# A dense product in Strassen form: units of 1024 tokens in place of 512, with half of each unit's squares kept and multiplied later

## The chip, the cores and the metric

The kernel runs on one core of one Trainium2 chip. The metric is the device time of one execution in microseconds (us); less is better. Four engines matter here: TensorE (PE, matmuls; its weight loads are shown apart as PEld), VectorE (DVE), ScalarE (ACT) and GpSimd (POOL). SyncE (SP) issues most transfers.

## The reference, cut to what matters

Three stages follow one another: a chunked attention, a mixture of experts that sends each token to one expert, and a dense feed-forward net over 3072 tokens. The change is in the third and in the few microseconds ahead of it.

```python
def _moe2_ref(x, w_in, w_out):        # x [3072, 512], w_in [512, 2048], w_out [2048, 512]
    h = x @ w_in
    r = np.maximum(h, 0.0)
    g = r * r
    return (g @ w_out).astype(np.float32)
```

## The kernel before, in words

Every large product is made in float32 precision from parts: an operand is split into a high part `hi` (a cast on ACT, L105) and a low part `lo` (a subtraction on DVE, L108), and a product is the three matmuls hi·hi, hi·lo and lo·hi (helper `split`).

**The experts.** A loop over slots `s` of 128 tokens (`for s in range(KE, NA)`, NA = 28) runs four groups of 12 matmuls a slot: `mm1(s+1, "a")`, `mm2(s, "a")`, `mm1(s+1, "b")`, `mm2(s, "b")`, with transposes (`htr`, `xtr`) between. Where a slot has another expert than the one before, the weights are split anew (`renew`). At the end of a slot `finish` scales the result (ACT, L1156) and GpSimd scatters its 128 rows to `y_d` in DRAM (L1157, indirect). Four times in a slot the loop calls `ffn_step`. In the last two slots (s = 26 and 27) each call takes one piece from the generator `ffn.run()`, so that the start of the third stage is woven into the experts. All queues run in the order in which the program issues; nothing is reordered later.

**The dense net.** The tokens, 24 tiles of 128 in expert order, are read back from `y_d` (`load_y`, L1257), transposed on PE (`ytr`, L1266), and multiplied by `w_in` in one level of Strassen's scheme: both operands are cut in quarters, seven products of sums of quarters replace eight. The tokens' seven sums (`sums`, L1279) are split into `yc1` to `yc7` (`ycw`). The weights' seven sums have been made and split earlier and lie in DRAM (`wi_d`); they are read back for each use (L1322).

Before, a unit `u` has 512 tokens (`NU` = 6), and a step (u, d), d from 0 to 3, makes 512 columns of the hidden layer. One of its seven products is 12 matmuls with 256 columns in the moving operand (L1313): two halves `jj` by two `kt` by three parts. The results lie in four PSUM banks X, Y, Z and W. ACT and DVE add them up (L1373 to L1401: `c1`, `u2`, `v`, `c2`), take `max(h,0)*h` (L1398, L1403) and split the square into `g` (`split_g`). `second(u, d, half)` then multiplies `g` by `w_out` (`mm2`, L1338 to L1340: 24 matmuls of 512 columns), one step behind the products, into four PSUM banks `acc`, one for each 128 tokens. After the last step of a unit `evict` copies them out, and GpSimd scatters the rows to `out` (L1360).

**Weights of the second product.** `w_out` comes as float64 and is converted in 32 pieces by `Convert`; each piece takes four DVE instructions (L190 to L199) and a split. Half of them are made in the experts' stage, and 16 are made after it, one at every second piece of the generator (`conv.step()`), so in the first four steps.

**The seam.** Between the experts and the dense net stands a branch, `tc.If(cnt > NA)` (L1603), for extra slots that these inputs do not need.

Of the kernel before, what the change touches and what calls it, by code (L numbers as in the profile page):

```python
# [21 lines left out]
def kernel(  # L22
# [33 lines left out]
    NU = NT // 4  # L56
# [1106 lines left out]
    class Ffn:  # L1163
# [3 lines left out]
        def __init__(self, wout, conv):  # L1167
            self.wout, self.conv = wout, conv
            self.w, self.yc, self.ys, self.yb, self.src, self.g, self.z = {}, {}, {}, {}, {}, {}, {}
            self.acc = None  # L1170
            self.out = []
# [26 lines left out]
        def combine(self, d, blocks):  # L1198
# [10 lines left out]
            def make(i):  # L1209
                t = self.w[i] = self.big.tile([P, 2, 2, 256], F32R, name="ww", tag=f"w{i}")  # L1210
                hi, lo = (t[:, x].rearrange("p k f -> p (k f)") for x in range(2))
                split(hi, lo, src[i])
                return t

            def store(i):
                r0 = (7 * d + i - 1) * P
                nc.sync.dma_start(out=wi_d[r0:r0 + P, :], in_=self.w[i].bitcast(F32).rearrange("p a k f -> p (a k f)"))
                return None
# [31 lines left out]
        def bank(self, b):  # L1250
            t = self.z[b] = self.ps.tile([P, 2, 256], F32, name="z" + b, tag="z" + b)
            return t

        def load_y(self, u, j):
            pool, tag = (moe.xp, "mx") if u == 0 or j < 2 else (moe.yp, "ysb")
            t = pool.tile([P, DM], F32R, name="ys", tag=tag)
            nc.sync.dma_start(out=t.bitcast(F32), in_=y_d[(4 * u + j) * P:(4 * u + j + 1) * P, :])  # L1257
            self.ys[u, j] = t

        def ytr(self, u, t):  # L1260
            for h in range(2):
                z = self.bank(("XY", "ZW")[h][t])
                for i in range(2):
                    for kt in range(2):
                        kk = 2 * h + kt
                        nc.tensor.transpose(  # L1266
                            z[:, kt, i * P:(i + 1) * P].bitcast(F32R),
                            self.ys[u, 2 * t + i][:, kk * P:(kk + 1) * P], identr,
                        )
                if (u, h) not in self.yb:  # L1270
                    pool, tag = (wres["1a"], ("wh1a1", "wl1a1")[h]) if u == 0 else (holds["2b"], f"r2b{h}")
                    self.yb[u, h] = pool.tile([P, 2, 512], F32, name="yb", tag=tag)
                nc.scalar.copy(out=self.yb[u, h][:, t], in_=z.rearrange("p a b -> p (a b)"))

        def sums(self, u):
            (b11, b12), (b21, b22) = ((self.yb[u, h][:, 0], self.yb[u, h][:, 1]) for h in range(2))
            t1, t2, t3, t4 = (self.big.tile([P, 512], F32, name=f"t{j}", tag=f"t{j}") for j in range(1, 5))
            for o, a, b in ((t1, b12, b11), (t2, b22, t1), (t3, b22, b12), (t4, b21, t2)):
                nc.vector.tensor_tensor(out=o, in0=a, in1=b, op=ALU.subtract)  # L1279
            self.src = {1: b11, 2: b21, 3: b22, 4: t4, 5: t1, 6: t2, 7: t3}  # L1280

        def ycw(self, *which):
            for i in which:
                t = self.yc[i] = self.big.tile([P, 2, 2, 256], F32R, name="yc", tag=f"yc{i}")
                hi, lo = (t[:, x].rearrange("p k f -> p (k f)") for x in range(2))
                split(hi, lo, self.src[i])

        def prep(self):
            self.load_y(0, 0)
            self.load_y(0, 1)  # L1290
            yield "load"
            self.ytr(0, 0)
            self.load_y(0, 2)
            self.load_y(0, 3)
            yield "x"
            self.ytr(0, 1)
            yield "x"
            self.sums(0)
            self.ycw(1, 6)
            yield "x"  # L1300
            self.ycw(5, 7)
            yield "x"
            self.ycw(2, 3, 4)
            yield "x"

        def product(self, u, d, i, b, start):
            z = self.bank(b) if start else self.z[b]
            w, y = self.w[i], self.yc[i]
            for jj in range(2):
                c = slice(jj * P, (jj + 1) * P)  # L1310
                for kt in range(2):
                    for x, (wx, yx) in enumerate(((0, 0), (0, 1), (1, 0))):
                        nc.tensor.matmul(  # L1313
                            out=z[:, jj, :], lhsT=w[:, wx, kt, c], rhs=y[:, yx, kt, :],
                            start=start and (jj, kt, x) == (0, 0, 0), stop=(jj, kt, x) == (1, 1, 2),
                            skip_group_check=True,
                        )
            if (u, d) != (NU - 1, ND - 1):
                d1 = (d + 1) % ND
                t = self.w[i] = self.big.tile([P, 2, 2, 256], F32R, name="ww", tag=f"w{i}")  # L1320
                r0 = (7 * d1 + i - 1) * P
                nc.sync.dma_start(out=t.bitcast(F32).rearrange("p a k f -> p (a k f)"), in_=wi_d[r0:r0 + P, :])  # L1322
            return z.rearrange("p a b -> p (a b)")

        def split_g(self, half, src):
            g = [wres["1a"].tile([P, 2, 2, 256], F32R, name="g", tag=f"w{x}1a{half}") for x in "hl"]
            split(*(z.rearrange("p t j c -> p (t j c)") for z in g), src.rearrange("p t c -> p (t c)"))
            self.g[half] = g

        def mm2(self, d, half, j):  # L1330
            gh, gl = self.g[half]
            t, c = j // 2, slice(j % 2 * P, (j % 2 + 1) * P)
            for jj in range(2):
                wt = self.wout[4 * d + 2 * half + jj]
                wh, wl = wt[:, 0], wt[:, 1]
                a, b_ = gh[:, t, jj, c], gl[:, t, jj, c]
                s0, s1 = (d, half, jj) == (0, 0, 0), (d, half, jj) == (ND - 1, 1, 1)
                nc.tensor.matmul(out=self.acc[j], lhsT=a, rhs=wh, start=s0, stop=False)  # L1338
                nc.tensor.matmul(out=self.acc[j], lhsT=a, rhs=wl, start=False, stop=False)  # L1339
                nc.tensor.matmul(out=self.acc[j], lhsT=b_, rhs=wh, start=False, stop=s1)  # L1340

        def second(self, u, d, half):
            if (d, half) == (0, 0):
                self.acc = [
                    pool.tile([P, DM], F32, name=f"acc{j}", tag=tag)
                    for j, (pool, tag) in enumerate(((moe.ps_h, "h"), (moe.ps_y, "y"), (moe.ps_t, "tr"), (moe.ps_t, "tr")))
                ]
            if u == 0:
                self.conv.until(8 * ND + 2 * (4 * d + 2 * half + 2))
            for j in range(4):  # L1350
                self.mm2(d, half, j)

        def evict(self, u, j):
# [5 lines left out]
            jj = 4 * u + j  # L1359
# [6 lines left out]

        def step(self, u, d):
# [293 lines left out]
```

## Time and profile before

| | |
|---|---|
| Three runs | 996.0, 999.01 and 999.05 us; median 999.01 us |
| The profiled execution | 998.1 us, of which the profile's span is 996.4 us |
| PE busy over the span | 957.3 us (96%) |
| DVE, ACT, POOL busy | 608.1, 396.6, 164.7 us |
| First matmul of a Strassen product | 475.7 us after the start of the span |
| Granted TensorE clock | 1.00 nearly throughout (2.4 GHz); 0.50 is 1.2 GHz |

Matmuls are pipelined: the time that one takes is longer than the distance to the next. What a stream of them costs is read from start to start in the timeline.

### The profile page before, as it was taken

Reading aid. Unit: us, or ns where it says so; the run is one execution under the profiler, and the core shown is the slowest. Engines: PE = TensorE matmul, PEld = TensorE weight load, DVE = VectorE, ACT = ScalarE, POOL = GpSimd, SP = SyncE. Lnnn points to the kernel's source line nnn. Section 1 sums busy time; section 2 is a strip of 40 time slices with the busy share of each in tenths; the row PEclk is TensorE's granted clock in tenths of the full one; section 3 lists DMA queues with packets and bytes.
Section 4 is the critical chain, followed back from the end, with each engine's and each line's share of the span. In section 5 each row is a group of like instructions: output and inputs, shape, how many; then the busy total and the mean of one; then the engine's idle time right before and its main releaser. Section 6 shows DMA issues by size and latency. Waiting matters only on the chain.

```text
span 996.4 us, 19267 instructions
## 1 busy us (share of the span) xinstructions
PE 957.3 (96%) x6990; PEld 827.1 (83%) x6990; DVE 608.1 (61%) x1163; ACT 396.6 (40%) x701; POOL 164.7 (17%) x197
## 2 busy tenths in 40 slices
PE   6889799999999999999999999999999999999997
PEld 5667577888887887877889999989989989899996
DVE  7777795647757677885797543633654454455333
ACT  8656533635546465675434212211321211132111
POOL 8765212121211111210000010010000001001001
PEclk9999799999999999999999999999999999999999
DMA  8993716554857677895895574575556557545621
GB/s 328 349 407 138 253 37 229 191 169 128 308 188 279 210 267 250 311 336 206 313 345 173 190 252 155 190 267 165 174 195 228 180 180 244 195 153 189 219 79 43
DMA packets 74600, 217.11 MB, mean 218 GB/s; under 512 B 8436, under 2 KB 8564, under 8 KB 74496
## 3 DMA queue, kind: packets, MB, share of 16 engines
q1 hardware_dynamic: 55488, 166.50, 47.8%
q0 software_dynamic: 8640, 28.32, 8.0%
q10 hardware_dynamic: 10368, 20.98, 6.3%
q8 instruction: 57, 0.93, 0.4%
q14 instruction: 47, 0.39, 0.1%
HBM read 257.70 MB, written 38.80 MB: 298 GB/s over the span
## 4 chain that ended last, share of the span: by engine, by line
issue 66%; DMA 15%; POOL 2%; POOLq 0%
DMA y_d<-ysb,sidx 15%; POOL out_dram L1360 2%; POOLq L1657 0%; POOLq L1031 0%; POOLq L1360 0%; POOLq L1157 0%; POOLq L1603 0%
## 5 line engine op out<-in xcount | busy, mean ns | idle before, releaser
L1340 PE MATMUL acc<-wo,g 128*128 128x512 f32 x384 | 149.9, 390 | 0.0
L1339 PE MATMUL acc<-wo,g 128*128 128x512 f32 x384 | 149.7, 390 | 0.0
L1338 PE MATMUL acc<-wo,g 128*128 128x512 f32 x384 | 149.5, 389 | 0.0
L1360 POOL DMA_INDIRECT out_dram<-osb,oid x24 | 25.5, 1062 | 485.1 <-ACT osb L1356 475.3
L1397 DVE TENSOR_TENSOR cf<-zY,v 128x512 f32<-128x512 f32 x24 | 16.6, 690 | 137.6 <-PE zY L1313 137.6
L105 ACT CAST g<-cf 128x1024 fp32r<-128x1024 f32 x48 | 50.6, 1054 | 118.2 <-DVE cf L1398 68.5
L108 DVE TENSOR_TENSOR g<-cf,g 128x1024 fp32r<-128x1024 f32 x48 | 58.8, 1225 | 60.6 <-ACT g L105 60.6
L1394 ACT COPY cf<-zX 128x512 f32<-128x512 f32 x24 | 14.1, 587 | 200.6 <-PE zX L1313 200.6
L1340 PEld LDWEIGHTS acc<-wo,g 128*128 128x128 f32 x384 | 72.1, 188 | 15.2
L1338 PEld LDWEIGHTS acc<-wo,g 128*128 128x128 f32 x384 | 72.3, 188 | 13.4
L1339 PEld LDWEIGHTS acc<-wo,g 128*128 128x128 f32 x384 | 72.1, 188 | 13.4
L1157 POOL DMA_INDIRECT y_d<-ysb,sidx x28 | 33.5, 1195 | 273.3 <-ACT ysb L1156 208.7
L1313 PEld LDWEIGHTS zX<-yc,ww 128*128 128x128 f32 x576 | 74.6, 189 | 3.5
L1313 PE MATMUL zY<-yc,ww 128*128 128x256 f32 x576 | 76.9, 283 | 0.0
L1313 PE MATMUL zW<-yc,ww 128*128 128x256 f32 x576 | 76.9, 283 | 0.0
L1313 PE MATMUL zX<-yc,ww 128*128 128x256 f32 x576 | 76.6, 282 | 0.0
L1313 PEld LDWEIGHTS zY<-yc,ww 128*128 128x128 f32 x576 | 72.6, 192 | 0.1
L1313 PEld LDWEIGHTS zW<-yc,ww 128*128 128x128 f32 x576 | 72.6, 192 | 0.0
L135 POOL COPY kw<-kt 64x672 f32<-64x672 f32 x62 | 51.5, 831 | 10.5 <-PE sp L277 8.2
L1108 PE MATMUL yps<-wh2a,hTha 128*128 128x512 f32 x112 | 46.2, 412 | 0.3 <-ACT ysb L1156 0.3
L108 DVE TENSOR_TENSOR hTlb<-tr,hThb 128x512 fp32r<-128x512 f32 x28 | 19.3, 689 | 43.1 <-ACT hThb L105 42.6
L1108 PE MATMUL hps<-wh1b,xT 128*128 128x512 f32 x104 | 42.9, 413 | 1.8 <-ACT ha L1125 1.8
(313 smaller groups left out, 2058.3 us busy)
## 6 DMA issues: line engine op xcount, KB each, us to landing
ww<-wi_d SPq DMA_DIRECT2D x161, 512.0 KB
r1a<-in_moe_w_dram SPq DMA_DIRECT2D x54, 512.0 KB
r1b<-in_moe_w_dram SPq DMA_DIRECT2D x54, 512.0 KB
r2a<-in_moe_w_dram SPq DMA_DIRECT2D x52, 512.0 KB
r2b<-in_moe_w_dram SPq DMA_DIRECT2D x52, 512.0 KB
wi_d<-ww SPq DMA_DIRECT2D x28, 512.0 KB
vb<-in_v_dram SPq DMA_DIRECT2D x32, 390.0 KB
rw<-in_moe_w_in_dram ACTq DMA_DIRECT2D x32, 256.0 KB
```

Of the source, the lines that this page charges most:

```text
L105: nc.scalar.copy(out=hi, in_=src)
L108: eng.tensor_tensor(out=lo, in0=src, in1=hi.bitcast(F32), op=ALU.subtract)
L135: (nc.vector if eng == "v" else nc.gpsimd).tensor_copy(out=out, in_=in_)
L1108: nc.tensor.matmul(out=out_ps, lhsT=ah, rhs=wh, start=first, stop=False)
L1157: nc.gpsimd.indirect_dma_start(out=y_d[:, :], out_offset=bass.IndirectOffsetOnAxis(ap=sidx[:, s:s + 1], axis=0), in_=y, in_offset=None, bo ...
L1313: nc.tensor.matmul(out=z[:, jj, :], lhsT=w[:, wx, kt, c], rhs=y[:, yx, kt, :], start=start and (jj, kt, x) == (0, 0, 0), stop=(jj, kt, x) ...
L1338: nc.tensor.matmul(out=self.acc[j], lhsT=a, rhs=wh, start=s0, stop=False)
L1339: nc.tensor.matmul(out=self.acc[j], lhsT=a, rhs=wl, start=False, stop=False)
L1340: nc.tensor.matmul(out=self.acc[j], lhsT=b_, rhs=wh, start=False, stop=s1)
L1360: ins = nc.gpsimd.indirect_dma_start(out=out[:, :], out_offset=bass.IndirectOffsetOnAxis(ap=oid[:, jj:jj + 1], axis=0), in_=o, in_offset=N ...
L1394: nc.scalar.copy(out=c1[:, 0], in_=z)
L1397: nc.vector.tensor_tensor(out=c1[:, 1], in0=z, in1=v, op=add)
```

## The change

1. A unit has 1024 tokens (`NU` = 3), and a step makes 256 columns of the hidden layer (128 of each half), so there are eight steps a unit and 24 in all, as before. A product is 6 matmuls with 512 moving columns (no `jj` loop), 168 products in all, as before.
2. A step's square has two token halves. The first is multiplied by `w_out` a step later, as before (`second`, 12 matmuls each). The second is kept in SBUF as float32 (`keep`, `kept`). After the eight steps `rest` splits the kept pieces one by one into two buffers and multiplies them: 16 pieces of 12 matmuls, in the same four PSUM banks.
3. The weights of two steps lie in one tile, so `wi_d` is read at every second step.
4. Transposes and sums of the next unit are made in `rest`, in two halves `r` (`ytr(u+1, r)`, `ycw(r)`), straight from PSUM; for the first unit they are made in the last two slots of the experts.
5. For that, the loop over slots takes the generator's first piece (the eight loads of `y_d`, issued on SP) at the end of slot 25, ahead of what slot 26 issues there, and then one piece a call: the transposes of r = 0 at the first call in slot 26, eleven sums and splits over the other three, the transposes of r = 1 at the first call in slot 27, and so on. No product is left in the experts' loop (before, two were).
6. The tiles for `w_out` get other places in SBUF; five in place of six are loaded at the first of the two places in slot 27.

```diff
-    NU = NT // 4
+    NU = NT // 8
...
+        def ycw(self, r):
+            b11, b12, b21, b22 = (self.b[h, t] for h in range(2) for t in range(2))
...
+            return [
+                lambda: nc.scalar.copy(out=tmp_tile("t1", "u2"), in_=b12),
+                lambda: sub(tmp_tile("t3", "v"), b22, tmp["t1"]),
+                lambda: sub(tmp["t1"], tmp["t1"], b11),
+                put(1, b11), put(7, "t3"), put(5, "t1"),
+                lambda: sub(tmp_tile("t2", "v"), b22, tmp["t1"]),
+                put(2, b21), put(6, "t2"),
+                lambda: sub(tmp_tile("t4", "u2"), b21, tmp["t2"]),
+                put(3, b22), put(4, "t4"),
+            ]
 
         def prep(self):
...
             self.load_y(0, 0)
             self.load_y(0, 1)
             yield "load"
...
+            for r in range(2):
+                self.ytr(0, r)
+                ops = self.ycw(r)
+                yield "x"
+                for n in (4, 4, 4):
+                    for _ in range(n):
+                        ops.pop(0)()
+                    yield "x"
 
         def product(self, u, d, i, b, start):
             z = self.bank(b) if start else self.z[b]
             w, y = self.w[i], self.yc[i]
-            for jj in range(2):
-                c = slice(jj * P, (jj + 1) * P)
-                for kt in range(2):
-                    for x, (wx, yx) in enumerate(((0, 0), (0, 1), (1, 0))):
-                        nc.tensor.matmul(
-                            out=z[:, jj, :], lhsT=w[:, wx, kt, c], rhs=y[:, yx, kt, :],
...
-            if (u, d) != (NU - 1, ND - 1):
...
+            for kt in range(2):
+                for x, (wx, yx) in enumerate(((0, 0), (0, 1), (1, 0))):
+                    nc.tensor.matmul(
+                        out=z, lhsT=w[:, d % 2, wx, kt], rhs=y[yx][:, kt, :],
...
+            if d % 2 and (u, d) != (NU - 1, 2 * ND - 1):
...
+            kept = (c1[:, 1], c2[:, 1]) if last else self.keep(d)
+            relu2(kept[0], c1[:, 1])
+            self.split_g(1, c2[:, 0])
+            relu2(kept[1], c2[:, 1])
...
+        def rest(self, u):
+            D, nxt = 2 * ND, u + 1 < NU
+            order = [(D - 1, 0), (D - 1, 1)] + [(d, half) for d in range(D - 1) for half in range(2)]
+            n = len(order)
+            self.second(u, D - 1, 0)
+            self.split_g(0, self.kept[order[0]])
+            for j in range(4):
+                self.mm2(1, D - 1, 1, j, False, True)
+                self.evict(u, 0, j)
+            self.split_g(1, self.kept[order[1]])
+            yield "x"
+            self.open_acc()
+            ops = []
+            for k in range(0, n - 2):
+                for j in range(4):
+                    self.mm2(k % 2, *order[k], j, k == 0, False)
+                self.split_g(k % 2, self.kept[order[k + 2]])
+                if nxt and k in (0, 7):
+                    r = int(k > 0)
...
+                    self.ytr(u + 1, r)
+                    ops = self.ycw(r)
...
+                else:
+                    for _ in range(2):
+                        if ops:
+                            ops.pop(0)()
+                yield "x"
+            for j in range(4):
+                for k in (n - 2, n - 1):
+                    self.mm2(k % 2, *order[k], j, False, k == n - 1)
+                self.evict(u, 1, j)
...
-            if s < NA - 2:
+            if s < NA - 3 or (s == NA - 3 and n < 2):
                 return
+            n = 1
...
             moe.mm2(s, "b")
-            ffn_step(1)
+            ffn_step(2)
```

## Rows read from the trace of the kernel before

**Rows 1.** The page: busy time of the engines, share, instructions.

```profile
PE 957.3 (96%) x6990; PEld 827.1 (83%) x6990; DVE 608.1 (61%) x1163; ACT 396.6 (40%) x701; POOL 164.7 (17%) x197
```

**Rows 2.** Busy time by stretch: length, then PE, PEld, DVE, ACT, POOL, clock, DMA.

```profile
457.30:483.50 26.20, 23.46 (x125) 18.98 (x123) 15.66 (x21) 15.63 (x27) 3.48 (x3) 1.00 0.70 241
483.50:508.00 24.50, 24.46 (x176) 23.25 (x177) 19.25 (x42) 7.47 (x15) 0.00 (x0) 1.00 0.91 348
568.00:650.00 82.00, 82.00 (x525) 74.61 (x524) 40.54 (x49) 19.71 (x29) 4.32 (x4) 1.00 0.61 204
896.00:990.00 94.00, 94.00 (x574) 84.59 (x573) 37.64 (x43) 17.40 (x24) 5.82 (x6) 1.00 0.38 131
```

**Rows 3.** Groups of instructions by shape, whole span (busy us, mean ns, idle before).

```profile
L1340 PE MATMUL acc<-wo,g 128*128 128x512 f32 x384 | 149.9, 390 | 0.0
L1313 PE MATMUL zY<-yc,ww 128*128 128x256 f32 x576 | 76.9, 283 | 0.0
L1313 PE MATMUL zZ<-yc,ww 128*128 128x256 f32 x288 | 38.5, 283 | 1.5 <-PEq L1603 1.5
L105 ACT CAST yc<-t 128x512 fp32r<-128x512 f32 x24 | 14.2, 620 | 6.8 <-DVE t L1279 6.7
L108 DVE TENSOR_TENSOR wl2a<-r2a,wh2a 128x1024 fp32r<-128x1024 f32 x16 | 18.8, 1217 | 2.4 <-ACT wh2a L105 2.4
```

**Rows 4.** Timeline of PE, two products and the matmuls behind them (start, us).

```profile
599.94 1.60 PE L1313 MATMUL zZ<-yc,ww 128*128 128x256 f32 x12
601.38 1.60 PE L1313 MATMUL zW<-yc,ww 128*128 128x256 f32 x12
603.51 0.39 PE L1338 MATMUL acc<-wo,g 128*128 128x512 f32 x1
...
605.55 0.39 PE L1338 MATMUL acc<-wo,g 128*128 128x512 f32 x1
```

**Rows 5.** Timeline and waits of SP's queue ahead of the loads of `y_d`.

```profile
458.96 0.55 SPq L1015 DMA_DIRECT2D r2b<-in_moe_w_dram  x2
461.52 0.35 SPq L1257 DMA_DIRECT2D ys<-y_d  x1
...
SPq L1257 <- DMA y_d<-ysb,sidx: 1.8, 1, 1.8
```

**Rows 6.** Timeline of PE in slots 26 and 27.

```profile
460.38 0.48 PE L1108 MATMUL yps<-wh2a,hTha 128*128 128x512 f32 x1
464.21 0.36 PE L1266 MATMUL zX<-identr,ys 128*128 128x128 f32 x2 [0.37 <-DMA ys<-y_d]
464.91 0.37 PE L1266 MATMUL zX<-identr,ys 128*128 128x128 f32 x2 [0.33 <-DMA ys<-y_d]
465.12 0.51 PE L1266 MATMUL zZ<-identr,ys 128*128 128x128 f32 x4
465.46 0.46 PE L1108 MATMUL hps<-wh1b,xT 128*128 128x512 f32 x1
483.54 1.66 PE L1313 MATMUL zZ<-yc,ww 128*128 128x256 f32 x12 [1.46 <-PEq L1603]
```

**Rows 7.** Timeline of DVE: two splits, one after the other; one converted piece.

```profile
479.46 0.69 DVE L108 TENSOR_TENSOR yc<-yb,yc 128x512 fp32r<-128x512 f32 x1
480.06 0.68 DVE L108 TENSOR_TENSOR yc<-t,yc 128x512 fp32r<-128x512 f32 x1
498.37 0.42 DVE L108 TENSOR_TENSOR wo<-wf,wo 128x256 fp32r<-128x256 f32 x1
500.03 0.69 DVE L1377 TENSOR_TENSOR u<-zY,cf 128x512 f32<-128x512 f32 x1
```

**Rows 8.** Timeline of PE behind an idle stretch, and a stretch's clock there.

```profile
152.73 0.50 PE L1108 MATMUL hps<-wh1b,xT 128*128 128x512 f32 x1 [1.81 <-ACT ha L1125]
154.50:155.00 0.50, 0.50 (x2) 0.39 (x2) 0.50 (x2) 0.00 (x0) 0.00 (x0) 0.50 1.07 418
157.50:158.00 0.50, 0.50 (x13) 0.50 (x12) 0.00 (x0) 0.18 (x1) 0.00 (x0) 0.84 1.05 389
```

More of the change, by code (lines that the diff above doesn't have):

```diff
@@ L1260, in ytr, with tiles, load_y @@
-        def ytr(self, u, t):
+        def tiles(self, r):
+            return [4 * t + 2 * r + i for t in range(2) for i in range(2)]
+        def load_y(self, u, r):
+            for n, j in enumerate(self.tiles(r)):
+                if u:
+                    t = (moe.xp if n < 2 else moe.yp).tile([P, DM], F32R, name="ys", tag="mx" if n < 2 else "ysb")
+                elif n % 2 == 0:
+                    kind = ("1a", "1b")[r]
+                    pair = holds[kind].tile([P, 2, DM], F32R, name="ys", tag=f"r{kind}{n // 2}")
+                    t = pair[:, 0]
+                else:
+                    t = pair[:, 1]
+                nc.sync.dma_start(out=t.bitcast(F32), in_=y_d[(8 * u + j) * P:(8 * u + j + 1) * P, :])
+                self.ys[u, j] = t
@@ L1270, in ytr @@
[L1270 to L1286, printed above, removed]
+                        for i in range(2):
+                            kk = 2 * h + kt
+                            nc.tensor.transpose(
+                                z[:, kt * 256 + i * P:kt * 256 + (i + 1) * P].bitcast(F32R),
+                                self.ys[u, 4 * t + 2 * r + i][:, kk * P:(kk + 1) * P], identr,
+                            )
@@ L1330, in mm2 @@
[L1330 to L1340, printed above, removed]
+            for kt in range(2):
+                for x, (wx, yx) in enumerate(((0, 0), (0, 1), (1, 0))):
+                    nc.tensor.matmul(
+                        out=z, lhsT=w[:, d % 2, wx, kt], rhs=y[yx][:, kt, :],
+                        start=start and (kt, x) == (0, 0), stop=(kt, x) == (1, 2),
+                        skip_group_check=True,
+                    )
@@ new lines, in windex, with mm2 @@
+        def windex(self, d, half):
+            return 4 * (d // 2) + 2 * half + d % 2
+        def mm2(self, n, d, half, j, first, last):
+            g, wt, c = self.g[n], self.wout[self.windex(d, half)], slice(j * P, (j + 1) * P)
+            nc.tensor.matmul(out=self.acc[j], lhsT=g[:, 0, c], rhs=wt[:, 0], start=first, stop=False)
+            nc.tensor.matmul(out=self.acc[j], lhsT=g[:, 0, c], rhs=wt[:, 1], start=False, stop=False)
+            nc.tensor.matmul(out=self.acc[j], lhsT=g[:, 1, c], rhs=wt[:, 0], start=False, stop=last)
@@ L1423, in run @@
         def run(self):
+            self.kept = {}
             yield from self.prep()
             for u in range(NU):
-                for d in range(ND):
+                for d in range(2 * ND):
                     yield from self.step(u, d)
-            self.second(NU - 1, ND - 1, 0)
-            for j in range(4):
-                self.mm2(ND - 1, 1, j)
-                self.evict(NU - 1, j)
-            yield "x"
+                yield from self.rest(u)
     with tc.manual_schedule():
```

162 lines of the change are left out of this document (80 added, 82 removed).

## The prediction

> **What bounds the kernel now.** Read the page's first part first: PE is busy for 96% of the span, DVE for 61%, ACT for 40% [rows 1]. Then look where that share is full. By stretch, PE is busy in every microsecond of the dense net, from the first product behind the branch to the last matmul, and the clock is at its upper level; DVE is half idle there, except in the first 25 us, where it is busy for 19.25 of 24.5 us [rows 2]. So in the dense net only what PE issues counts, as long as no other engine comes late. The stretch ahead of it, the last two slots of the experts, is the one with holes: 23.46 of 26.2 us [rows 2], with waits for loads of `y_d` and for the branch [rows 6]. The change touches both: it shortens the issue in the full stretch and reorders the one with holes.
>
> What a product costs is read from start to start in the timeline, not from the mean durations, which overlap [rows 3]. Twelve 256-column matmuls take 601.38 - 599.94 = 1.44 us, 120 ns each; nine of 512 columns take 605.55 - 603.51 = 2.04 us, 227 ns each [rows 4]. Two small ones cost 240 ns, one large one 227 ns.
>
> **The products.** 2016 matmuls of 256 columns (three groups of 576 and one of 288, [rows 3]) become 1008 of 512. A product goes from 1.44 us to 6 x 0.2267 = 1.36 us; 168 products save 168 x 0.08 = 13.4 us. No row has a 512-column matmul with `yc` and `ww`, but those with `g` and `wo` have the same type, shape and a weight load each, so I take their distance. The bounds are no gain (0, if weight loads still set the pace) and 13.4 us. `second` and `rest` together keep the 1152 matmuls of before (3 x 384), and the 96 transposes stay 96.
>
> Here a rule of the Trainium skill speaks against the gain: "TensorE: Matmul & The Clock Gate", section "Back-to-back issue gap", gives an isolated matmul N / 2.4 ns and a fixed part of about 2.5 ns. By that rule 1008 fewer matmuls would save an estimated 1008 x 2.5 ns = 2.5 us. The rows give a fixed part of 2 x 120 - 227 = 13 ns, so the trace does not agree, and the sum goes by the rows.
>
> **The loads of `y_d` move ahead.** They wait for the scatter of slot 25: SP's loads begin at 461.52, after a wait on that scatter [rows 5]. That is no earlier in the new order, since the scatter is not. But PE reaches the transposes earlier: in the new order they stand where `mm2(26, "a")` stands now, at 460.38, and the first tile was there at 464.21, the second at 464.91 [rows 6]. The half r = 0 needs four tiles; at 0.7 us each the fourth comes at 464.2 + 3 x 0.7 = 466.3. Eleven transposes follow it, at 0.34 / 4 us each (465.12 to 465.46, [rows 6]), so PE goes on at 467.3. That is 6.9 us for 1.36 us of work: a stall of 5.5 us. Moving the eight loads also delays what SP issues next, the reload of `r2b` (458.96 now, [rows 5]), to about 465; it is split only in slot 27, 15 us later, so it costs nothing unless it needs over 10 us to land.
>
> **The sums of both halves fall into the experts' loop.** Before, these slots hold 11 DVE instructions for the first unit (four sums, seven splits); now they hold two lots of 11, with one copy and seven casts each on ACT. DVE needs 0.60 us from one to the next (480.06 - 479.46, [rows 7]). PE's order from 467.3: three groups of 12 matmuls at 12 x 0.2267, some 2.8 us with their starts, and two lots of transposes at 0.35 us; it reaches the transposes of r = 1 at 476.5. These write the banks that the sums of r = 0 still read. DVE's order: the split for `htr(27, "a")` at 471.3, three instructions and a put (0.6 x 4 = 2.4), the weights `wl2a` (two at 1.2, [rows 3]), then seven more up to the last reader of bank W (4.2): 480.2. So PE waits about 2.7 us in the midst of these transposes and goes on at 480.5. Two groups of the experts follow (5.5 us, to 486.0), then the branch, where PE sat 1.46 us [rows 6]: the first product starts at 487.5. By then DVE has done the first split of r = 1 (about 485.8) and reaches that for the second product at 488.8, just in time.
>
> Now compare equal work. At 483.54 the kernel before had two products behind it (2.9 us) and 16 transposes fewer (1.34 us). The seam thus costs 487.5 - 483.54 + 2.9 - 1.34 = 5.5 us. The bounds are 2.8 us, if DVE is not late at the second transposes, and about 8 us, if the second loads or the reload are late too.
>
> **The clock.** PE idles 3.8 us before the first tile, and again 2.7 us. Behind an idle 1.81 us at 152.73 the granted clock stood at 0.50 from about 154.2 until about 157.7 [rows 8]: 3.5 us at the lower level, a loss of 1.75 us of full-rate work. Behind the 1.46 us at the branch it stayed at 1.00 [rows 2]. I take 1.3 us for the first gap, because a part of the slow time falls on waiting anyway, and 1.0 for the second (little over an even chance of 1.75): 2.3 us, between 0 and 5.
>
> **Conversions and squares in the first unit.** A step has now 11 DVE instructions of 512 elements, 6.6 us, and five conversions a step, each 500.03 - 498.37 = 1.66 us [rows 7]: 14.9 us, against 7 x 1.36 + 24 x 0.2267 = 15.0 us of PE. Before it was 20.5 us of PE for a little more work. The first step has no `second`: 9.5 us of PE against 6.6 + 3 x 1.66 = 11.6 us of DVE. DVE falls some 2 us behind and does not catch up before the conversions end in the fourth step. PE needs DVE's sums of the products 6 and 7 only behind `second`, some 4 to 5 us later, so most of the lag is covered. I take 1.0 us, between 0 and 6 (all that DVE can lose to casts queued on ACT behind a wait).
>
> **`rest`.** While PE does 12 matmuls (2.72 us), DVE has one split and up to two sums or splits (1.8 us); ACT up to three casts of 0.62 us [rows 3], under 1.9 us. The split of piece k+2 starts when piece k is multiplied, and has the 2.72 us of piece k+1 to get ready; it takes about 1.4 us. Hidden, cover 1.3 us a piece. The transposes for the next unit wait for loads issued some 50 us (r = 0) or seven pieces (r = 1) earlier: nothing. The reads of `wi_d` halve, and each has a whole step to land: nothing. Evictions and the tail behind the last matmul have the same form: nothing.
>
> **Sum.** -13.4 + 5.5 + 2.3 + 1.0 = -4.6 us. From the profiled execution's 998.1 us that is 993.5 us (span about 992); the median of the runs shown stands 0.9 us above that execution, so 994.4 us.
>
> **The rivals.**
> 1. *The seam is cheap.* DVE is not late at the second transposes and the clock holds: 2.8 us in place of 5.5 and 2.3, nothing in the first unit. -13.4 + 2.8 gives 988.4 us. For it: the clock has held through 1.46 us idle. Against it: 3.8 us idle is more than twice the stretch behind which it fell. Chance 0.19.
> 2. *DVE bounds the first unit.* The 14.9 against 15.0 us leave no room for bubbles, and ACT's casts stand behind copies that wait for PE. With 1.2 us lost in each of the four steps beyond the forecast's 1.0, the time is 999.2 us, no change. Against it: DVE may lag 4 to 5 us first. Chance 0.14.
> 3. *`rest` is not covered (slower).* If the split and the two sums of a piece run as a chain, cast (0.62), then subtraction (0.69), three times, a piece takes 3.9 in place of 2.72 us. It decides from 0.32 us for each of the 24 pieces in the two units that prepare another (7.6 us undo the gain and the 0.3%); at the full 1.2 us the time is 1023 us, at a third of it 1004. Against it: ACT can cast ahead while DVE subtracts, as the two successive splits 0.60 us apart show [rows 7]. Chance 0.08.
> 4. *The wide product is no faster.* If the columns alone set the pace, a 512-column matmul costs as much as two narrow ones and the 8.8 us of the seam, the clock and the first unit remain: 1007.8 us. By the fixed part that the section of the Trainium skill's page "TensorE: Matmul & The Clock Gate" cited above gives, the time would be an estimated 1005.3 us. Against it: 227 ns stands for all 1152 matmuls of `second` in this trace, 13 ns under two narrow ones. Chance 0.03.
>
> **How the numbers follow.** The forecast has 0.56, with its own range 991 to 997.5. About 0.3% (3 us) is what a measurement of this kernel can tell from no change. Faster by more (under 996): most of the forecast (0.47) and rival 1, 0.66. Within: the rest of the forecast and rival 2, 0.23. Slower: rivals 3 and 4, 0.11. A range of 989 to 999.5 us leaves out half of rival 1 and rivals 3 and 4, about 0.2.
>
> **What would show it.** Right: products at 1.36 us from start to start; a PE wait for `ys` of 3 to 6 us near 460 and one for DVE near 478; a clock under 1.00 behind the first; the first product at 487 to 491; no PE wait in `rest`; a last matmul near 986. Wrong: products at 1.44 us (rival 4), PE waits for `g` on DVE or ACT beyond 600 us (rival 3), PE waits for `u2`, `cf` or `g` over 5 us in all in the first four steps (rival 2), or a clock of 1.00 all through the seam (rival 1).

## The result and the profile after

The changed kernel takes 1008.31 us (median of seven runs, 1005.85 to 1010.84), the one before 999.05 us (seven runs, 996.0 to 1003.65): a ratio of 1.0089, 95% interval 1.0063 to 1.0115. It is 0.9% slower. The forecast was 994.4 us with a range up to 999.5; the time lies outside.

The profiled execution has a span of 1006.6 us against 996.4 before. First the page's busy times of the changed kernel, the answer to [rows 1]:

```profile
PE 956.9 (95%) x5982; PEld 778.7 (77%) x5982; DVE 622.1 (62%) x1259; ACT 397.3 (39%) x731; POOL 162.6 (16%) x197
```

The 1008 matmuls that were to go have gone, yet PE is busy as long as before: what was saved in number was lost again in slower matmuls. The span grew by waits. The waits of PE from slot 26 to the fourth step (line, releaser, us in total, times, longest):

```profile
PE zX L1277 <- DMA ys<-y_d: 3.9, 2, 3.6
PE zZ L1277 <- DVE tu L1291: 3.5, 1, 3.5
PE zX L1336 <- PEq L1662: 2.5, 1, 2.5
PE zY L1277 <- DMA ys<-y_d: 2.4, 2, 2.1
PE zW L1336 <- DVE cf L1418: 0.9, 2, 0.5
PE tr L1132 <- ACT hb L1125: 0.3, 1, 0.3
```

The kernel before waited 0.9 us there for `y_d` and 1.46 us at the branch. The timeline of PE there (start, us, idle before), the answer to [rows 6]:

```profile
455.45 0.39 PE L1108 MATMUL hps<-wh1a,xT 128*128 128x512 f32 x1
...
462.34 0.37 PE L1277 MATMUL zX<-identr,ys 128*128 128x128 f32 x1 [3.56 <-DMA ys<-y_d]
463.02 0.62 PE L1277 MATMUL zX<-identr,ys 128*128 128x128 f32 x3 [0.31 <-DMA ys<-y_d]
465.75 0.37 PE L1277 MATMUL zY<-identr,ys 128*128 128x128 f32 x1 [2.10 <-DMA ys<-y_d]
...
467.85 0.76 PE L1108 MATMUL yps<-wh2a,hTha 128*128 128x512 f32 x1
...
483.56 0.72 PE L1277 MATMUL zZ<-identr,ys 128*128 128x128 f32 x4 [3.55 <-DVE tu L1291]
...
494.73 0.47 PE L1336 MATMUL zX<-yc,ww 128*128 128x512 f32 x1 [2.50 <-PEq L1662]
```

The first product was forecast at 487.5 and starts at 494.73. Equal work: the kernel before goes from the start of slot 26's `mm1` (457.30) to its third product (483.54) in 26.24 us, with two products (2.88) done and 16 transposes (1.34) not yet; the changed one takes 494.73 - 455.45 = 39.28 us to its first. The rows of the kernel before:

```profile
457.30 0.39 PE L1108 MATMUL hps<-wh1a,xT 128*128 128x512 f32 x1
475.94 1.59 PE L1313 MATMUL zX<-yc,ww 128*128 128x256 f32 x12
480.50 0.40 PE L1313 MATMUL zY<-yc,ww 128*128 128x256 f32 x2
```

The seam costs 39.28 - 26.24 + 2.88 - 1.34 = 14.6 us in this execution. Experiments 1, 2, 5 and 11 leave the seam as it is; their traces have 37.1, 38.0, 38.4 and 38.5 us, so that it costs 12.4 to 14.6 us. The windows (busy time of PE, PEld, DVE, ACT and POOL, then the clock and DMA) show where part of it is:

```profile
467.80:471.70 3.90, 3.90 (x12) 3.08 (x12) 0.00 (x0) 0.00 (x0) 0.00 (x0) 0.52 0.23 91
482.00:487.00 5.00, 3.44 (x14) 2.96 (x15) 4.69 (x8) 4.05 (x7) 0.51 (x1) 0.50 0.44 176
495.30:498.70 3.40, 3.40 (x10) 2.62 (x9) 0.78 (x2) 1.37 (x4) 0.00 (x0) 0.52 0.21 71
```

Behind each of the three long stalls (for `y_d`, for DVE, at the branch) the clock stands at its lower level, 1.2 GHz, and a matmul takes 0.43 us from start to start in place of 0.23. Now the products, in the timeline of PE, where [rows 4] had 1.44 us:

```profile
593.27 0.39 PE L1336 MATMUL zY<-yc,ww 128*128 128x512 f32 x1
...
594.66 0.39 PE L1336 MATMUL zW<-yc,ww 128*128 128x512 f32 x1
...
596.06 0.39 PE L1357 MATMUL acc<-wo,g 128*128 128x512 f32 x1
...
598.84 0.39 PE L1336 MATMUL zX<-yc,ww 128*128 128x512 f32 x1
```

A product takes 594.66 - 593.27 = 1.39 us (1.40 for the next), not 1.36, and the 12 matmuls of `second` take 2.78 us, not 2.72. The medians for products 1 to 7, from start to start over the whole trace, are 1.382, 1.392, 1.387, 1.399, 1.387, 1.391 and 1.368 us.

At the end of each of the three `rest` something was lost too. Waits of PEld from 500 us on (the kernel before has none there), and PE at the end of the first `rest`:

```profile
PEld acc L1357 <- ACT g L105: 1.5, 3, 0.5
PEld acc L1359 <- DVE g L108: 1.3, 3, 0.4
660.93 0.39 PE L1359 MATMUL acc<-wo,g 128*128 128x512 f32 x1
661.40 0.50 PE L1357 MATMUL acc<-wo,g 128*128 128x512 f32 x1
661.74 0.39 PE L1358 MATMUL acc<-wo,g 128*128 128x512 f32 x1
```

There the last two pieces alternate, and the split of the last one has only three matmuls (0.7 us) to get ready in. Four matmuls take 1.5 us in place of 0.9, at 660.93, 829.68 and 995.58: 1.8 us in all.

**The balance.** Behind the fourth step, where no wait and no low clock stretches it, a product takes 1.437 us in the mean before and 1.386 after: 168 x 0.051 = 8.6 us gained. Against it stand 0.9 us for the slower `acc` pitch (0.2284 against 0.2276 us, 1152 matmuls), 1.65 for the low clock in the first two products, 1.5 from start to start for the waits in the first steps, and 1.8 at the ends of `rest`: 2.75 us are left. Equal stretches of the dense net (508.9 us before from first product to last matmul, without the branch, slot 27's `mm2` and the 16 transposes; 506.2 after) say 2.7. Then 14.6 for the seam, and -1.85 because slot 26 began that much earlier in this execution: 10.0 us, against 10.2 us between the spans.

### The profile page after: what moved, and what is told of

It is laid out like the page before. It is cut to its first block, busy times and chain, and to the rows that moved or that the text cites. A ratio compares the mean times of both kernels' runs of the same rounds, so it can differ in the third digit from the quotient of the medians.

```text
span 1006.6 us, 17170 instructions
## 1 busy us (share of the span) xinstructions
PE 956.9 (95%) x5982; PEld 778.7 (77%) x5982; DVE 622.1 (62%) x1259; ACT 397.3 (39%) x731; POOL 162.6 (16%) x197
## 5 line engine op out<-in xcount | busy, mean ns | idle before, releaser
L1402 DVE SCALAR_TENSOR_TENSOR cf<-cf 128x512 f32<-128x512 f32 x54 | 37.1, 692 | 76.8 <-ACT cf L1425 75.9
L105 ACT CAST g<-cf 128x512 fp32r<-128x512 f32 x54 | 33.5, 621 | 105.7 <-PE acc L1359 74.6
L1336 PE MATMUL zX<-yc,ww 128*128 128x512 f32 x192 | 68.3, 397 | 2.5 <-PEq L1662 2.5
L1336 PE MATMUL zW<-yc,ww 128*128 128x512 f32 x192 | 67.9, 394 | 0.9 <-DVE cf L1418 0.9
L108 DVE TENSOR_TENSOR g<-gk,g 128x512 fp32r<-128x512 f32 x42 | 29.1, 693 | 63.9 <-ACT g L105 63.3
L1336 PE MATMUL zY<-yc,ww 128*128 128x512 f32 x192 | 68.3, 397 | 0.0
L108 DVE TENSOR_TENSOR g<-cf,g 128x512 fp32r<-128x512 f32 x54 | 37.4, 692 | 31.9 <-ACT g L105 31.2
L105 ACT CAST g<-gk 128x512 fp32r<-128x512 f32 x42 | 26.1, 623 | 73.9 <-PE acc L1359 73.9
L135 POOL COPY kw<-kt 64x672 f32<-64x672 f32 x62 | 51.4, 829 | 10.2 <-PE sp L277 7.6
L1109 PE MATMUL yps<-wl2a,hTha 128*128 128x512 f32 x112 | 45.5, 406 | 0.0
L1110 PE MATMUL yps<-wh2a,hTla 128*128 128x512 f32 x112 | 45.4, 405 | 0.0
```

Source lines behind the costliest of these rows:

```text
L105: nc.scalar.copy(out=hi, in_=src)
L108: eng.tensor_tensor(out=lo, in0=src, in1=hi.bitcast(F32), op=ALU.subtract)
L135: (nc.vector if eng == "v" else nc.gpsimd).tensor_copy(out=out, in_=in_)
L1109: nc.tensor.matmul(out=out_ps, lhsT=ah, rhs=wl, start=False, stop=False)
L1110: nc.tensor.matmul(out=out_ps, lhsT=al, rhs=wh, start=False, stop=last)
L1336: nc.tensor.matmul(out=z, lhsT=w[:, d % 2, wx, kt], rhs=y[yx][:, kt, :], start=start and (kt, x) == (0, 0), stop=(kt, x) == (1, 2), skip_g ...
```

## The experiments

Slot 26 begins between 455.5 and 460.7 us in the traces, whatever the kernel. So runs of one time are compared from the start of slot 26's `mm1` (the seam, 39.3 us in the changed kernel) and from the first product on (the dense stretch, 506.2 us).

**1. The tiles on the right side moved by 32 bytes.** Why is a product 1.39 and not 1.36 us long?

```diff
+ctx.enter_context(tc.tile_pool(name="pad", bufs=1, side="right")).tile([P, 8], F32, name="pad")
```

> The changed kernel with 32 bytes a partition set aside at the top of SBUF, so that every buffer allocated from that end (g, w_out, most of the low parts of the tokens' sums, the kept squares) moves down by 32 bytes; nothing else changes. In the changed kernel those buffers start at addresses that leave 32 when divided by 64, while the buffers from the other end (yc, ww and two of the low parts) start at multiples of 64. Only product 7, whose three operands all lie at the one end, and pieces of the second product that have run for a while, reach 227 ns from matmul to matmul; the other products take 231 to 232 ns. Theory A (a stream of matmuls whose operands change between the two alignments is slower): with one alignment all products take 1.36 us and 12 matmuls of the second product 2.72 us, so the time falls by 168 x 0.03 + 42 x 0.06 = 7 to 8 us. Theory B (it is the distance in SBUF, or the switch between the two products itself): products stay at 1.39 us and the time stays within 1 us.

1006.22 us (before 998.99; ratio 1.0073, 1.0055 to 1.0092). Products behind the fourth step take 1.379 us in the mean (1.386 without the 32 bytes), the dense stretch is 1.6 us shorter. The place has an effect, far from 7 us, and it does not only help: product 7 went from 1.368 to 1.383, though its own operands did not move. Nor is it enough that all operands lie at one end, as those of products 1 and 7 do: product 1 takes 1.382 us with and without the 32 bytes.

**2. The product in 12 matmuls of 256 columns again, in the new units.**

```diff
-            for kt in range(2):
-                ...rhs=y[yx][:, kt, :]
+            for jj in range(2):
+                c = slice(jj * 256, (jj + 1) * 256)
+                for kt in range(2):
+                    ...rhs=y[yx][:, kt, c]
```

> The changed kernel with each product made by twelve matmuls of 256 columns again, two column halves one after the other; everything else stays (units of 1024 tokens, the run of kept squares, the seam). It prices the wide product alone. The prediction's term: a product goes back from 1.36 to 1.44 us, plus 13 us. What the changed kernel's trace shows (1.39 us a product): plus 8 us, less up to 2 us if the second product's first matmuls no longer run slow. If operands from the two ends of SBUF also slow the narrow matmuls, a product takes more than 1.44 us and the difference is more than 10 us.

A product behind the fourth step takes 1.427 us, the dense stretch 511.6 us. So the wide product is worth 168 x 0.041 = 6.9 us by the products alone, and 5.4 us of the dense stretch: waits and low clock in the first steps cost 3.1 us with the wide products and 1.7 with the narrow ones. The other 1.7 us of the 8.6 came without the wider matmul, since the narrow products took 1.437 us in the kernel before. The total, 1017.5 us, holds a slot 26 that began 5 us later.

**3. The loads of the second half behind the first transposes.**

```diff
             self.load_y(0, 0)
-            self.load_y(0, 1)
             yield "load"
             for r in range(2):
                 self.ytr(0, r)
+                if r == 0:
+                    self.load_y(0, 1)
```

> The changed kernel with the loads of the second four token tiles (r = 1) issued only after the transposes of the first four, instead of all eight at once. In the changed kernel the first two tiles came 2.8 and 3.4 us after the first issue, the third and fourth only after 6.2 and 6.9 us. Theory A (the eight loads share the bandwidth, so that the third and fourth tile wait for the last four): the third and fourth tile come by 4.2 to 4.9 us, PE's second wait for ys falls from 2.1 us to under 0.5 us, and the seam is about 2 us shorter. Theory B (each load has its place in the queue, and the third is late for another reason, the reload that follows for instance): the second wait stays at about 2 us.

1008.0 us. The wait for the third tile falls from 2.10 to 1.30 us, that for the first stays at 3.44; the seam is 38.2 us. But in the traces of 1, 2, 5 and 11, where all eight loads are issued at once as in the changed kernel, the wait for the third tile is 0.98, 0.64, 1.08 and 1.88 us. So the 0.8 us lie within what executions differ by: neither theory is shown, and what makes the third tile late stays open.

**4. The same, and the first transposes one call later.**

```diff
             yield "load"
+            yield "x"
             for r in range(2):
```

> As the run before it in this list, and in addition the transposes of the first half stand one call later, behind mm2 of slot 26 and the transposes that follow, so that PE has 3.1 us of other work while the tiles come. Theory A (the seam's loss is PE standing at an early transpose, and each such idle stretch costs a fall of the clock as well): PE's waits for ys fall from 6.3 us to about 1.5 us, the granted clock stays at 1.00 until slot 27, and the first product starts 4 to 6 us earlier after slot 26 begins than in the changed kernel. Theory B (the seam is bound by the chain of sums on DVE, 22 instructions and four split weights behind the last slots): the waits for ys fall but the wait for DVE ahead of the second transposes grows by as much, and the first product starts within 1.5 us of where it did.

1004.4 us, the seam 33.6 us. The timeline of PE (with the gaps):

```profile
463.04 0.28 PE L1277 MATMUL zX<-identr,ys 128*128 128x128 f32 x1 [0.31 <-DMA ys<-y_d]
...
465.26 0.28 PE L1277 MATMUL zY<-identr,ys 128*128 128x128 f32 x1 [1.12 <-DMA ys<-y_d]
...
481.41 0.50 PE L1277 MATMUL zZ<-identr,ys 128*128 128x128 f32 x4 [1.24 <-DVE tu L1291]
...
493.11 0.50 PE L1338 MATMUL zY<-yc,ww 128*128 128x512 f32 x1 [1.71 <-ACT yc L105]
```

The waits for `y_d` shrink from 6.3 to 2.2 us, the one for DVE from 3.55 to 1.24: a group of 12 matmuls ahead of the transposes covers them. But 1.71 us come back at the second product, where the later sums of the second half are now late, and the clock still falls (0.50 from 467 to 472).

**5. The left places given to other products.** The low parts `yl1` and `yl2` lie at the left end of the core's memory, those of the other products at the right end.

```diff
-self.low = dict(zip((1, 7, 5, 2, 6, 3, 4), [(self.big, "yl1"), (self.big, "yl2")] + wr + ...
+self.low = dict(zip((3, 4, 5, 2, 6, 1, 7), [(self.big, "yl1"), (self.big, "yl2")] + wr + ...
```

> The low parts at the left end of SBUF (yl1, yl2), which products 1 and 7 read in the changed kernel (1.382 and 1.368 us each product), go to products 3 and 4 (1.387 and 1.399 us there), and 1 and 7 get the places of 3 and 4 at the right end; nothing else is changed. Theory A (the pitch depends on where in SBUF the operands of neighbouring matmuls lie): products 3 and 4 fall to 1.365 to 1.375 us, product 7 rises to about 1.387. Theory B (the pitch follows what ran before and the fixed order of the passes, not the place): each product keeps its time within 0.005 us. By both the total stays within 1 us of the changed kernel (1008.3 us).

Products 3 and 4 fall from 1.387 and 1.399 to 1.360 and 1.368 us, 7 rises from 1.368 to 1.399, 1 from 1.382 to 1.392; 2, 5 and 6 keep theirs. Products 3 and 4 in the timeline of PE:

```profile
610.97 0.39 PE L1336 MATMUL zY<-yc,ww 128*128 128x512 f32 x1
...
612.33 0.39 PE L1336 MATMUL zW<-yc,ww 128*128 128x512 f32 x1
...
613.70 0.39 PE L1357 MATMUL acc<-wo,g 128*128 128x512 f32 x1
```

That is theory A, though product 7 rose more than it said. The 1.36 us of the forecast exist, where the operands lie well. The dense stretch is 505.8 us, 0.4 shorter; the total, 1010.45 us, holds a slot 26 that began 3.5 us later.

**6 and 7. Loads two calls earlier, transposes behind work** (7 with the 32 bytes).

```diff
             self.load_y(0, 0)
+            yield "load"
             self.load_y(0, 1)
             yield "load"
             ...
                 ops = self.ycw(r)
-                yield "x"
                 for n in (4, 4, 4):
                 ...
+                if r == 0:
+                    yield "x"
+                    yield "x"
 ...
                 moe.mm1(s + 1, "b")
-            ffn_step(1)
+            ffn_step(2)
```

> The y loads of the first half are issued one call of the unit ahead of the end of scatter 25, those of the second half one call later still, and the first transposes stand two calls later, so that the transposes of both halves come more than 10 us after their loads and behind a slot product; no step of DVE is dropped. Theory A (the seam's three kinds of loss, 6.3 us of waits for y, 3.55 us for DVE and the falls of the clock behind them, all come from where the loads and transposes stand): no wait for y, no wait of the second transposes for DVE, the clock stays at 1.00 from the start of slot 26's mm1 to the first product, the seam costs 14 us less, and the total is 993 to 997 us, below the kernel before (999.0). Theory B (the loads share the queue and the rate with slot 26's own weights, so that loads issued earlier push other waits in): the wait returns at mm1 or mm2 of slots 25 to 27, and the total is 1001 to 1008 us.

> The same, with 32 bytes for each partition allocated first on the right side, so that the tiles on that side begin at another place. Theory A (the place sets a part of the pitch): 1.5 to 2 us less than without these 32 bytes, as in the run that had them alone. Theory B (that difference was one between runs): the same within 0.7 us.

6: 997.42 us (before 997.95; ratio 0.9995, 0.9978 to 1.0013): level with the kernel before, and by the ratios 0.94% (9.4 us) less than the changed one. That is just outside theory A's 993 to 997 us. 7: 994.86 us (0.9965, 0.9944 to 0.9985). The waits of PE in 6, and two windows:

```profile
PE zX L1339 <- PEq L1665: 2.7, 1, 2.7
PE yps L1108 <- ACT ysb L1156: 2.6, 1, 2.6
PE zW L1339 <- DVE cf L1421: 0.9, 2, 0.5
```

```profile
455.70:479.50 23.80, 21.09 (x118) 17.37 (x116) 17.00 (x23) 13.75 (x24) 1.96 (x2) 1.00 0.75 266
482.40:486.00 3.60, 3.60 (x10) 2.92 (x11) 2.43 (x4) 1.61 (x4) 0.01 (x1) 0.59 0.17 55
```

No wait for `y_d`, none for DVE at the second transposes, and the clock holds through the slots: theory A on these points. The seam is 26.6 us, 12.7 shorter than in the changed kernel's trace (10.5 to 11.9 shorter than in the other four), not 14: a new wait of 2.6 us stands in slot 27, where the eviction of slot 26's output is queued on ACT behind a cast that waits for DVE, and the clock still falls behind the branch. The 32 bytes give 2.6 us between the two medians (2.4 us in the dense stretch). Of these, 0.6 lie in the first four steps, where the clock did not fall behind the branch in this trace (1.00 from 483.7 to 486).

**8. PE kept busy in the waits.** 39 dummy matmuls are added, whose result nobody reads: 16 and 8 in the waits for `y_d`, 15 in the one for DVE.

```diff
+fill = {(0, 0, 0): 16, (0, 0, 1): 8, (1, 1, 0): 15}.get((r, h, t), 0) if u == 0 else 0
+for n in range(fill):
+    nc.tensor.matmul(out=dummy..., lhsT=w[:, 0, 0:P], rhs=w[:, 0], start=n == 0, stop=n == fill - 1)
```

> The changed kernel with dummy matmuls whose result nobody reads: 16 ahead of the first y transposes, 8 ahead of the second group and 15 ahead of the transposes of bank Z in slot 27, so that TensorE is busy while it would wait; the waits end when they did. Theory A (the clock that falls behind these waits costs about 4 us in the two slot products behind them and in the first products): the granted clock is 1.00 from 457 to 500 us, mm2 of slots 26 and 27 runs at 0.23 us a pitch instead of 0.43, the first product starts 3 to 5 us earlier than in the changed kernel (39.3 us behind the start of slot 26's mm1), and the total is 1003 to 1006 us. Theory B (the waits alone are the cost): the first product starts where it did within 1 us.

The windows of the seam (clock third from the right):

```profile
461.00:470.00 9.00, 8.60 (x47) 6.81 (x46) 0.69 (x1) 0.75 (x2) 0.00 (x0) 1.00 0.82 283
470.00:482.00 12.00, 11.76 (x61) 9.57 (x60) 8.31 (x12) 7.26 (x12) 0.98 (x1) 1.00 0.52 190
482.00:490.00 8.00, 7.36 (x36) 5.58 (x35) 7.08 (x10) 5.24 (x9) 0.00 (x0) 1.00 0.66 238
```

The clock holds at 1.00 throughout. The time is 1004.1 us; the seam is 32.0 us, 7.3 shorter with 39 matmuls more in it. Each `mm2(s, "a")` takes 2.8 us where it took 4.5 (467.85 to 472.39) and 4.6: 3.5 us are the clock, and some 0.5 in the transposes beside them. The rest came with it: the wait at the branch was gone too (0.58 us for DVE in place of 2.50; 12 has more on this), and the tiles of `y_d` came 1 us sooner, within the spread that 3 names. Theory B is out.

**9. The last four sums behind that eviction, the first product ahead of the branch** (on top of 7).

```diff
-                for n in (4, 4, 4):
+                for n in (4, 4, 0, 4, 0) if r == 0 else (4, 4, 4):
 ...
+        next(chunks)
         cnt = nc.values_load(cnt_i[0:1, 0:1], min_val=0, max_val=NS)
```

> The kernel of the run before with early loads and 32 bytes of offset, with two more edits: the last four sums of the first half are issued behind the eviction of slot 26's output instead of ahead of it, and the first product is issued ahead of the branch on the number of slots. Theory A (what is left in the seam are two waits of 2.6 us, one for that eviction, which stood behind these sums on ACT, one for TensorE's sequencer at the branch): both go, the first product starts 22 to 24 us behind the start of slot 26's mm1 (26.1 without these edits), and the total is 990 to 993 us, 0.5 to 0.9% under the kernel before. Theory B (the waits move: the second half's sums are then late for the first products): the first product starts earlier but waits of the same size stand in the first two steps, and the total stays at 994 to 996 us.

995.89 us (before 999.55; ratio 0.9960, 0.9944 to 0.9975), by its ratio level with 7. The first product came after 23.5 us as hoped, but the second did not follow it (timeline of PE, then one row of DVE):

```profile
479.06 0.47 PE L1336 MATMUL zX<-yc,ww 128*128 128x512 f32 x1 [1.09 <-DVE yl L108]
...
480.29 0.40 PE L1336 MATMUL zX<-yc,ww 128*128 128x512 f32 x1
484.52 0.47 PE L1336 MATMUL zY<-yc,ww 128*128 128x512 f32 x1 [3.83 <-ACT wo L105]
481.40 0.69 DVE L108 TENSOR_TENSOR yl<-tv,yc 128x512 fp32r<-128x512 f32 x1
```

The edit for the eviction worked (0.3 us left of 2.6). The wait ahead of the first product became one of 3.83 us ahead of the second: the total came out almost as theory B has it. Its reason was wrong: it is not the sums, for the low part of the second product's operand was ready at 482.1 us (the row of DVE), 2.4 us ahead of the product.

**10. The same with the exchange of 5.**

> The same with the left places given to the low parts of products 3 and 4, as in the run that did only this. Theory A (a product whose low part lies at the left end takes less whatever the offset at the right end): products 3 and 4 take 1.360 to 1.370 us, 1 and 7 stay at 1.38, and the total is 0 to 1 us less. Theory B (the offset has already taken what the place costs): all products stay within 0.005 us of the run without it.

996.46 us (0.9969, 0.9953 to 0.9985): no gain. The wait at the same place carries the sequencer's name here (3.5 us). With the 32 bytes in place, product 4 takes 1.371 us, 3 takes 1.389, 1 takes 1.368: both theories miss. The places cannot be priced one by one.

**11. 1024 bytes in place of 32**, on the changed kernel.

> The changed kernel with 1024 bytes for each partition allocated first on the right side, in place of 32. The tiles there begin 1024 bytes lower, at the same place within any 64, 128, 256 or 512 bytes as in the changed kernel. Theory A (with the 32 bytes it was the alignment to 64 that helped): the products stay at 1.387 to 1.393 us mean as in the changed kernel, acc pitch 228.4 ns. Theory B (any move helps or harms by chance, through the distance between the operands): the products differ from that by more than 0.005 us.

All seven product medians are those of the changed kernel to the nanosecond, `acc` too (0.2284 us); 1009.4 us. So far theory A: a shift by 1024 bytes changes nothing, one by 32 bytes does.

**12. The number of slots loaded ahead of the slots**, without the early product of 9.

```diff
         pending = [None]
+        cnt = nc.values_load(cnt_i[0:1, 0:1], min_val=0, max_val=NS)
         for s in range(KE, NA):
 ...
-        next(chunks)
-        cnt = nc.values_load(cnt_i[0:1, 0:1], min_val=0, max_val=NS)
```

> The kernel of the last sums behind the eviction and the 32 bytes, without the product ahead of the branch; in its place the number of slots is loaded into the engines' registers ahead of the run of slots, so that only the branch itself stands ahead of the first product. Theory A (the 2 to 4 us at TensorE's sequencer are the load of the register): the first product waits for DVE at most, starts 22 to 24 us behind the start of slot 26's mm1, no wait of the second product, total 990 to 993 us. Theory B (they are the branch, the code behind it): a wait of 2 to 4 us for the sequencer stays ahead of the first product, total 994 to 996 us.

995.44 us (before 999.2; ratio 0.9960, 0.9934 to 0.9986). The timeline of PE around the branch, DVE's split for the first product, and the DMA queue q8 from 484.0 to 485.1 (one transfer of 16 KB):

```profile
482.42 0.39 PE L1110 MATMUL yps<-wh2b,hTlb 128*128 128x512 f32 x1
486.82 0.63 PE L1336 MATMUL zX<-yc,ww 128*128 128x512 f32 x1 [4.01 <-PEq L1663]
487.24 0.63 PE L1336 MATMUL zX<-yl,ww 128*128 128x512 f32 x1
483.07 0.69 DVE L108 TENSOR_TENSOR yl<-zX,yc 128x512 fp32r<-128x512 f32 x1 [0.65 <-ACT yc L105]
q8 instruction: 1, 0.02, 5.5%
```

The wait for the sequencer is still there with the load gone, 4.0 us long, and the split was done at 483.8: theory B, it is the branch. The matmuls behind it run at the lower clock.

The traces also show what ends the wait. The queue q8 carries instructions; in the dense net one of its transfers comes for some 250 instructions of PE and PEld. Here one starts at 484.10 and takes 0.96 us, and the next follows only 3.6 us later. The first matmul behind the branch starts 1.75 us after the first of them ends. In the traces of 13 of the 14 kernels, the one before among them, that distance is 1.59 to 1.83 us, while the wait ahead of the matmul goes from 0.56 us (experiment 4, where the transfer ended 1.2 us before PE's work did) to 4.0. In 8 alone no transfer falls in the 7 us ahead of the first product, and the wait there is for DVE. So the length of the wait goes by when these instructions come. Why the transfer begins 1.3 us behind the end of PE's last matmul here, and 2.3 us ahead of it in 4, is open.

The Trainium skill, "Runtime: NRT & Kernel Launch", section "Instruction fetch mechanics", says that a taken branch can break the sequential fetch of instructions and stall the engine until the target has been fetched. The waits and the transfers agree with that.

## Why the prediction was wrong

**The loads of `y_d`: half right.** The first tile came 2.77 us after the loads' first issue, the second 0.68 us later, as forecast. The step "at 0.7 us each the fourth comes at 464.2 + 3 x 0.7 = 466.3" failed: it took the distance of two tiles, and the third came 2.7 us behind the second (1.3 to 2.3 in the other four traces with these loads). Whether eight loads at once are the reason is not shown (experiment 3). The loads' first issue moved with the start of slot 26, from 461.52 [rows 5] to 459.57, so the earlier start is no part of it. The stall forecast at 5.5 us was 8.0 us (458.5 to 467.85, with 1.36 us of work).

**DVE at the second transposes: right in kind, short in size.** 2.7 us forecast, 3.55 us measured, at the place named. Experiment 6 removes both waits and with them 10.5 to 12.7 us of the seam: that they and what follows from them are most of the loss is shown.

**The clock: mis-sized.** Two falls were forecast at 2.3 us together. There were three. The two in the slots cost about 4 us (experiment 8), the one in the first products 1.65. The step that priced none behind the branch ("Behind the 1.46 us at the branch it stayed at 1.00") failed: the wait there was 2.50 us, and the clock fell behind it.

**The branch: missed.** I kept its 1.46 us [rows 6]. In the kernel before, the first product stood between slot 27's two `mm2` and the second behind the last of them; in the changed kernel no product stands ahead of the branch, and the wait was 2.50 us, up to 4.0 in experiment 12. The transfer of instructions that ends it began at 481.02 in the kernel before, 1.1 us ahead of the end of PE's work, and at 492.06 in the changed one, 0.2 us ahead. Experiment 9 shows that one product ahead of the branch doesn't shorten the wait.

So the terms +5.5 (seam) and +2.3 (clock) of the sum were 14.6, which holds the two falls in the slots, and 1.65. By the parts: 5.4 us more wait for `y_d` than before, 3.55 for DVE, 1.0 more at the branch, and 4.6 that are left, which the two slow `mm2` (3.5) and the slow transposes fill.

**The products: right in direction, two thirds in size.** The step "I take their distance", that of the matmuls with `g` and `wo`, failed: 0.051 us a product were saved, not 0.08, 8.6 us and not 13.4, and 7.7 with what the `acc` pitch lost. Of the 8.6 the wide matmul itself brought 6.9 (experiment 2). Experiments 1, 5 and 11 show that the pitch depends on where operands lie; no layout tried gives all products 1.36. Why is open: the exchange moved just the products whose low parts moved, but the 32 bytes also moved product 7, whose operands stayed.

The Trainium skill's rule that was weighed in the prediction ("TensorE: Matmul & The Clock Gate", "Back-to-back issue gap") made the gain an estimated 2.5 us. It is stated there for an isolated matmul, and the stream measured here has 6.9: the estimate was too low and my reading of the rows too high. The same section's N / 1.2 ns for the lower clock gives 427 ns for 512 columns; the trace agrees (468.40 to 471.39 in seven, 0.427 us each).

**The first unit: right. `rest`: right but for its end.** The first steps lost 1.5 us to waits from start to start (1.0 forecast), and PE was busy for 12.00 of 12 us in pieces of `rest` (628 to 640). The step that gives each split "the 2.72 us of piece k+1" failed at the last piece, where it had 0.7 us: 1.8 us in all, put at nothing. Rivals 2 and 3 did not happen; the cheap seam of rival 1 (2.8 us) is near what experiment 6 makes of it (26.61 - 26.24 + 2.88 - 1.34 = 1.9 us). That the time is near rival 4's (1007.8 us) is chance: the wide product was faster, the seam dearer.

With the seam mended (experiments 7, 9 and 12) the change is worth 0.35 to 0.4% against the kernel before. All three have the 32 bytes, and without them (6) it is level; what 32 bytes would do to the kernel before was not run. A wait of 2.0 to 4.0 us at the branch stands in all three.

## What to carry to other kernels

When work is woven into another loop, count for each of its pieces what must be behind it (load, sums, free banks), and place it at least a group of matmuls later; here earlier loads and later transposes (experiment 6) turned a loss of 0.9% into no loss. An idle gap of PE is priced with the slow matmuls behind it, which here cost 5.7 us beside 12.3 us of waits. When two streams of pieces are woven at the end of a loop, see how much work still covers the last piece. And take the pitch of a matmul from its own operands in their own places: of the 13 ns that the rows promised for each wide matmul, 8.5 came.

## What the runs showed of the hardware that was not expected

- The pitch of a 512-column matmul lay between 227 and 233 ns with the places of its operands: 32 bytes of shift changed product 7 by 15 ns (2.5 ns a matmul), 1024 bytes changed no product by as much as a nanosecond.
- PE waited 0.56 to 4.0 us at the branch, 4.0 with the load of the register moved far ahead of it. In 13 of 14 traces the first matmul behind it started 1.59 to 1.83 us after the end of a 16 KB transfer on the instruction queue q8.
- The length of an idle stretch alone did not decide the clock: behind 2.64 us in slot 27 of experiment 6 it stayed at 1.00, behind 2.67 us at the branch of the same trace it fell (0.59 from 482.4 to 486).
